# Mixing the MLP's two products tile by tile, with the second product one batch older

## The chip, the cores and the metric

One core of a Trainium2 chip runs the whole program. The metric is the device time of one execution in microseconds (us); each number quoted for a kernel is the median of its runs. Every run comes with the mean granted clock of TensorE (1.0 is full speed) and a state; for comparisons only runs of state "fast" are used (on one core, a run is slow when it is over 1.5% above the fastest of the same kernel). Ratios are computed as the mean time of one kernel's fast runs over the mean of the other's from the same rounds, so a ratio is not quite that of the two medians beside it.

## The reference

Attention with an added one in the softmax denominator, for 8 batches, 12 heads, 448 positions and 64 dimensions, followed by an MLP with a squared ReLU over the 3,584 resulting tokens.

```python
scores = scale * np.matmul(q, k.transpose(0, 1, 3, 2))
m = np.max(scores, axis=-1, keepdims=True)
e = np.exp(scores - m)
attn = e / (np.sum(e, axis=-1, keepdims=True) + np.exp(-m) + 1e-09)
attn_out = np.matmul(attn, v)
x = attn_out.transpose(0, 2, 1, 3).reshape(B * S, H * D)      # 3584 x 768
h = x @ w_in                                                  # 768 x 2048
r = np.maximum(h, 0.0)
out = (r * r) @ w_out                                         # 2048 x 768
```

## The kernel before

Attention runs in units of one batch and two heads, six units per batch (batch 0 has twelve, each of a part of the query positions). The MLP takes blocks of tokens: 128 and 256 from batch 0, then 512 and 384 in turn. While batch b's attention runs, TensorE also does the MLP of finished tokens: its matmuls are laid in five portions between the parts of each unit. A generator yields after each matmul, and `drain` takes matmuls from it until the portion's nanoseconds are used up.

```python
    def mlp_in(t0, n):                     # first product: 6 matmuls fill one PSUM tile (n >= 384)
        ...
        for f0 in range(0, NFFB, per):
            hp = m_psum.tile([128, 512], FP32, name="mp")
            ...                            # matmuls from win and xt, a yield after each
            nc.vector.tensor_scalar(out=rt[:, 0:m], in0=hp[:, 0:m], scalar1=0.0, scalar2=None, op0=ALU.max)
            nc.vector.tensor_mul(g[:, 0:m], rt[:, 0:m], rt[:, 0:m])

    def mlp_out(t0, n):                    # second product: 16 matmuls fill one PSUM tile
        ...
                op = m_psum.tile([128, 512], FP32, name="mp")
                ...                        # matmuls from g and wout, a yield after each
                nc.scalar.activation(out=ot[:, n0:n1], in_=op[:, 0:n1 - n0], func=AF.Copy, scale=OUT_SCALE)

    def drain(ns):
        while work and ns > 0:
            got = next(work[0], None)
            if got is None:
                work.pop(0)
            else:
                ns -= got
                left[0] -= got
    ...
    for i in range(NU + 1):                # one pass: scores of unit i, the rest of unit i - 1
        scores(u, et, 0)                   # first score group
        drain(share * 0.45)
        scores(u, et, 1)                   # second score group
        rcp = row_sums(prev, pes)
        values(prev, pet, xp, 0); values(prev, pet, xp, 1)
        drain(share * 0.15)
        for step in range(3):
            add_chunks(u, et, es, step)    # VectorE: sums of the exponentials
            drain(share * (0.15, 0.1, 0.15)[step])
        normalise(prev, xp, rcp)           # VectorE: writes one of xt's six chunks
        if i - 1 in ready:                 # a batch's last unit: its MLP becomes work
            for part in ready[i - 1]:
                queue(*part)
            share = left[0] / NPAIR
```

The pool `m_psum` has two buffers, shared by both products: a third tile can only begin when one of the two has been read out ("evicted"). VectorE evicts the first product (but for block 0), ScalarE the second; ScalarE also does all exponentials. I call the six passes that work on one block's MLP a stage.

The names in the profile lines: `qk` and `vn` are attention's operands, `sp` the scores, `et` their exponentials, `es` sums of these, `zp` the row sums, `rcp` their reciprocals, `xp` the values and `xt` the normalised output; `mp` is a tile of either product, `rt` and `g` its ReLU and the square, `ot` the output.

The softmax here doesn't subtract the row's maximum and nothing guards it: scores larger than these inputs give would overflow.

## Time and profile before

| | before |
|---|---|
| median time | 448.77 us (448.7 with later runs of the same rounds) |
| span in the profile | 445.8 us |
| TensorE busy, idle | 426.6 us, 19.2 us |
| TensorE's waits for VectorE's evictions of the first product | 5.3 us (4.8 + 0.5) |
| TensorE's waits for ScalarE's evictions of the second product | none |

TensorE's busy time is not its time at peak, and its idle time is real: a matmul that waits for a semaphore is not counted as busy. (A stop of a few tenths of a us can hide behind the end of the matmul before it, which the profile models.) In a kernel whose TensorE is 96% busy, the list of what TensorE waited for is the place to look, and the order in time around each wait says why it waited.

### The profile page before, as it was taken

Reading aid. Unit: us, or ns where it says so; the run is one execution under the profiler, and the core shown is the slowest. Engines: PE = TensorE matmul, PEld = TensorE weight load, DVE = VectorE, ACT = ScalarE, POOL = GpSimd, SP = SyncE. Lnnn points to the kernel's source line nnn. Section 1 sums busy time; section 2 is a strip of 40 time slices with the busy share of each in tenths; the row PEclk is TensorE's granted clock in tenths of the full one; section 3 lists DMA queues with packets and bytes.
Section 4 is the critical chain, followed back from the end, with each engine's and each line's share of the span. In section 5 each row is a group of like instructions: output and inputs, shape, how many; then the busy total and the mean of one; then the engine's idle time right before and its main releaser. Section 6 shows DMA issues by size and latency. Waiting matters only on the chain.

```text
span 445.8 us, 7533 instructions
## 1 busy us (share of the span) xinstructions
PE 426.6 (96%) x3147; PEld 228.7 (51%) x3147; DVE 244.7 (55%) x487; ACT 247.8 (56%) x361; POOL 33.8 (8%) x52
## 2 busy tenths in 40 slices
PE   8978899999999999999999989999999999999996
PEld 3556554544455545554455544654455545554454
DVE  3767683378722775258832487248662377428700
ACT  2888767754456646674456745764455655650011
POOL 8441100010000100010000100030000000000000
PEclk9999999999999999999999999999999999999999
DMA  9999999199021991279312793039902200010022
GB/s 171 197 197 204 208 202 197 52 191 216 1 64 46 198 179 33 71 124 207 79 37 71 116 217 79 37 62 206 178 1 72 71 1 1 37 37 35 1 71 71
DMA packets 78946, 47.22 MB, mean 106 GB/s; under 512 B 50624, under 2 KB 74944, under 8 KB 78528
## 3 DMA queue, kind: packets, MB, share of 16 engines
q0 software_dynamic: 24608, 22.40, 31.8%
q1 hardware_dynamic: 54304, 24.34, 23.9%
q8 instruction: 24, 0.39, 0.4%
q14 instruction: 10, 0.08, 0.1%
HBM read 45.71 MB, written 19.32 MB: 146 GB/s over the span
## 4 chain that ended last, share of the span: by engine, by line
PE 74%; DVE 17%; ACT 3%; issue 2%; DMA 2%; POOL 1%; ACTq 0%; POOLq 0%
PE mp L279 34%; PE mp L256 20%; PE xp L222 7%; PE sp L186 7%; DVE rt L265 7%; DVE es L199 4%; DVE g L267 3%; PE zp L230 3%; DMA kn<-in_k_dram 2%; ACT et L154 2%; PE sp L174 2%; DVE es L201 1%; DVE xt L242 1%; ACT lnz L233 1%; PE mp L146 1%
## 5 line engine op out<-in xcount | busy, mean ns | idle before, releaser
L154 ACT ACTIVATE et<-sp 112x896 f16<-112x896 f32 (+2 forms) x192 | 166.2, 913 | 125.4 <-PE sp L186 103.9
L256 PE MATMUL mp<-xt,win 128*128 128x512 f16 (+3 forms) x864 | 159.1, 332 | 8.3 <-DVE rt L265 4.8
L279 PE MATMUL mp<-wout,g 128*128 128x512 f16 (+1 forms) x896 | 154.2, 326 | 0.8 <-DVE rt L265 0.5
L256 PEld LDWEIGHTS <-win 128*128 128x128 f16 x864 | 77.3, 98 | 82.8 <-issue 25.7
L279 PEld LDWEIGHTS <-g 128*128 128x128 f16 x896 | 84.2, 98 | 64.6 <-issue 11.5
L199 DVE TENSOR_TENSOR es<-et 112x896 f16<-112x896 f16 x84 | 51.5, 621 | 106.3 <-ACT et L154 106.3
L265 DVE TENSOR_SCALAR rt<-mp 128x512 f16<-128x512 f32 (+1 forms) x120 | 76.0, 633 | 46.2 <-PE mp L256 43.5
L283 ACT ACTIVATE ot<-mp 128x512 f32<-128x512 f32 (+1 forms) x56 | 27.3, 487 | 64.5 <-PE mp L279 63.8
L267 DVE TENSOR_TENSOR g<-rt 128x512 f16<-128x512 f16 (+1 forms) x124 | 49.5, 399 | 7.0 <-ACT rt L263 2.8
L222 PE MATMUL xp<-et,vn 112*64 112x448 f16 (+2 forms) x432 | 45.5, 332 | 0.0
L186 PE MATMUL sp<-qk 64*112 64x224 f16 x576 | 42.8, 268 | 0.0
L186 PEld LDWEIGHTS <-qk 64*112 64x112 f16 x576 | 26.9, 127 | 25.4 <-issue 25.4
L233 ACT ACTIVATE lnz<-zp,one_b 128x448 f32<-128x448 f32 (+2 forms) x54 | 32.2, 596 | 1.9 <-PE zp L230 1.9
L242 DVE TENSOR_TENSOR xt<-xp,rcp 128x448 f16<-128x448 f32 (+2 forms) x54 | 30.5, 565 | 2.7 <-ACT rcp L234 2.7
L234 ACT ACTIVATE rcp<-lnz 128x448 f32<-128x448 f32 (+2 forms) x54 | 28.9, 535 | 1.7
L222 PEld LDWEIGHTS <-vn 112*64 112x64 f16 x432 | 24.0, 110 | 10.2 <-issue 0.2
L79 POOL DMA_DIRECT2D vn<-in_v_dram x10 | 8.9, 889 | 252.4 <-PE xp L222 239.6
L201 DVE TENSOR_TENSOR es<-es 112x896 f16<-112x896 f16 x42 | 26.2, 623 | 1.0
L230 PE MATMUL zp<-es,ones 112*64 112x448 f16 (+2 forms) x108 | 19.4, 356 | 1.0 <-DVE es L207 0.9
L174 PE MATMUL sp<-qk 64*112 64x192 f16 (+2 forms) x144 | 16.8, 308 | 1.6 <-ACT et L154 1.3
L363 PE MATMUL mp<-warm 128*128 128x512 f16 x31 | 10.7, 444 | 1.2 <-DVE warm L301 1.2
L174 PEld LDWEIGHTS <-qk 64*112 64x112 f16 x144 | 6.8, 124 | 9.4 <-issue 6.5
(32 smaller groups left out, 80.3 us busy)
## 6 DMA issues: line engine op xcount, KB each, us to landing
out_dram<-ot SPq DMA_DIRECT2D x12, 384.0 KB, 2.4
vn<-in_v_dram POOLq DMA_DIRECT2D x6, 672.0 KB, 8.8
stage_q<-in_q_dram POOLq DMA_DIRECT2D x5, 676.0 KB, 10.9
stage_k<-in_k_dram POOLq DMA_DIRECT2D x5, 676.0 KB, 13.7
win<-in_moe_w_in_dram POOLq DMA_DIRECT2D x8, 384.0 KB, 14.6
wout<-in_moe_w_out_dram POOLq DMA_DIRECT2D x4, 768.0 KB, 20.4
out_dram<-ot SPq DMA_DIRECT2D x8, 288.0 KB, 2.6
out_dram<-ot SPq DMA_DIRECT2D x8, 192.0 KB, 2.7
```

Of the source, the lines that this page charges most:

```text
L154: nc.scalar.activation(out=out_, in_=in_, func=AF.Exp, scale=scale)
L174: nc.tensor.matmul(sp[:, h, o:o + n], qk[r, 1, x + P * kk:x + P * kk + P], qk[r, 0, x + q0:x + q0 + n], start=True, stop=True)
L186: nc.tensor.matmul(sp[:, odd, h * (S // 2):(h + 1) * (S // 2)], qk[r, which, kx:kx + 2 * P - 1:2], qk[r, 0, x:x + S // 2], start=True, sto ...
L199: nc.vector.tensor_add(f[:, step], e[:, 2 * step], e[:, 2 * step + 1])
L222: nc.tensor.matmul(xp[64 * h:64 * h + 64, 0:n], vns[b][:, 2 * pr + h, kk, :], of_head(chunk(et, u, c, kk), u, h), start=(kk == 0), stop=(k ...
L230: nc.tensor.matmul(zp[64 * h:64 * h + 64, 0:n], ones, of_head(total, u, h), start=True, stop=True)
L233: nc.scalar.activation(out=lnz[:, 0:n], in_=zp[:, 0:n], func=AF.Ln, bias=one_b)
L242: nc.vector.tensor_mul(xts[b // 2][:, pr, c:c + n], xp[:, 0:n], rcp[:, 0:n])
L256: nc.tensor.matmul(hp[:, j * n:(j + 1) * n], win[:, dc, fb * 128:(fb + 1) * 128], xt[:, dc, x0:x0 + n], start=(dc == 0), stop=(dc == DCH - 1))
L265: nc.vector.tensor_scalar(out=rt[:, 0:m], in0=hp[:, 0:m], scalar1=0.0, scalar2=None, op0=ALU.max)
L267: nc.vector.tensor_mul(g[:, 0:m], rt[:, 0:m], rt[:, 0:m])
L279: nc.tensor.matmul(op[:, 0:n1 - n0], gt[fb][:, ts * 128:(ts + 1) * 128], wout[:, fb, n0:n1], start=(fb == 0), stop=(fb == NFFB - 1))
```

## The change

The intent is to spread VectorE's load: in place of a run of first-product tiles and then a run of second-product tiles, the tiles alternate. The second product needs all of a block's first product, so it comes from the block one batch older. Boilerplate is cut; every `yield` also gets a flag that marks the end of a tile.

```diff
+    def mixed(parts):
+        gens = [[0.0, total, gen] for gen, total in parts]
+        while gens:
+            g = min(gens, key=lambda g: g[0] / g[1])
+            for ns, end in g[2]:
+                g[0] += ns
+                yield ns
+                if end:
+                    break
+            else:
+                gens.remove(g)
...
-    ready = {NPAIR - 1: [(1, 0, 128)],
-             2 * NPAIR - 1: [(1, 128, 256), (2, 0, 128), (2, 128, 256)]}
-    t0 = 384
+    ready = {NPAIR - 1: [(1, 0, 128)], 2 * NPAIR - 1: [(1, 128, 256), (2, 0, 128)]}
+    last, t0 = (2, 128, 256), 384
     for b in range(1, B):
         n = 384 if b % 2 == 0 else 512
-        ready[(b + 2) * NPAIR - 1] = [(1, t0, n), (2, t0, n)]
+        ready[(b + 2) * NPAIR - 1] = [(1, t0, n), last]
+        last = (2, t0, n)
         t0 += n
...
-                for part in ready[i - 1]:
-                    queue(*part)
+                queue(ready[i - 1])
...
+    queue([last])
     drain(1e12)
```

More of the change, by code (lines that the diff above doesn't have):

```diff
@@ L258, in mlp_in @@
                     if j < per - 1 or dc < DCH - 1:
-                        yield n / 2.4
+                        yield n / 2.4, False
             m = per * n
@@ L269, in mlp_in @@
                 gt.append(g[:, j * n:(j + 1) * n])
-            yield n / 2.4
+            yield n / 2.4, True
     def mlp_out(t0, n):
@@ L281, in mlp_out @@
                     if fb < NFFB - 1:
-                        yield (n1 - n0) / 2.4
+                        yield (n1 - n0) / 2.4, False
                 nc.scalar.activation(out=ot[:, n0:n1], in_=op[:, 0:n1 - n0], func=AF.Copy, scale=OUT_SCALE)
                 if n1 < DM:
-                    yield (n1 - n0) / 2.4
+                    yield (n1 - n0) / 2.4, True
             c = t0 + ts * 128
@@ L296, in mlp_out @@
                 c += m
-            yield (DM - 512) / 2.4
+            yield (DM - 512) / 2.4, True
     warm = consts.tile([128, 512], FP16)
@@ L326, with queue @@
     work, left = [], [0.0]
-    def queue(part, t0, n):
-        work.append((mlp_in if part == 1 else mlp_out)(t0, n))
-        left[0] += (NFFB * DCH * n if part == 1 else n // 128 * NFFB * DM) / 2.4
+    def mixed(parts):
[9 more added lines that the diff above has]
+                gens.remove(g)
+    def queue(parts):
+        both = []
+        for part, t0, n in parts:
+            total = (NFFB * DCH * n if part == 1 else n // 128 * NFFB * DM) / 2.4
+            both.append(((mlp_in if part == 1 else mlp_out)(t0, n), total))
+            left[0] += total
+        work.append(mixed(both))
     def drain(ns):
```

## The prediction

> **What bounds the kernel now.** I read the page first, then the busy time by stage, the waits of TensorE stage by stage, the chain of waits, and the instructions in order of time around each wait. The page's engine line and the slices:
>
> ```profile
> PE 426.6 (96%) x3147; PEld 228.7 (51%) x3147; DVE 244.7 (55%) x487; ACT 247.8 (56%) x361; POOL 33.8 (8%) x52
> ...
> PE   8978899999999999999999989999999999999996
> ...
> DMA  9999999199021991279312793039902200010022
> ```
>
> TensorE is busy in 426.6 of 445.8 us, so a reordering can win at most the 19.2 us of idle time, and much of that is at the two ends. The DMA row matters later: the engines are full for the first seven slices (78 us), while weights, the first batches and the staged copy of batch 2 arrive.
>
> The busy time by stage (stretch, its length, then PE, PEld, DVE and ACT busy) shows where the idle time is:
>
> ```profile
> 0.00:44.00 44.00, 37.19 (x425) 22.65 (x425) 27.48 (x73) 31.74 (x51) 20.11 (x30) 1.00 1.30 192
> 44.00:90.00 46.00, 43.66 (x344) 25.24 (x342) 26.33 (x50) 33.62 (x50) 3.64 (x6) 1.00 0.92 162
> 90.00:145.00 55.00, 54.42 (x367) 27.34 (x366) 29.80 (x55) 29.75 (x42) 1.07 (x2) 1.00 0.53 105
> 145.00:194.00 49.00, 47.59 (x365) 26.04 (x363) 28.17 (x59) 30.68 (x44) 2.65 (x6) 1.00 0.57 110
> ...
> 421.00:446.00 25.00, 20.70 (x128) 12.27 (x126) 1.05 (x2) 3.92 (x8) 0.00 (x0) 0.98 0.20 64
> ```
>
> 6.8 us are lost before 44 us, 2.3 to 90 us, 4.3 at the very end (the last eviction and its store), and only 0.58 or 1.41 us in each middle stage, alternately for a block of 512 and of 384 tokens. What the idle time waits for, over the whole run:
>
> ```profile
> PE mp L256 <- DVE rt L265: 4.8, 13, 0.6
> ...
> PE mp L279 <- DVE rt L265: 0.5, 1, 0.5
> ```
>
> These 5.3 us are what mixing can win: the first product's PSUM tiles come one after another with two buffers, and VectorE, which also does the attention's additions, is sometimes late with an eviction. From 84 us on the waits by stage are 0.3 us in each 512 stage and 1.2 us in each 384 stage, three of each: 4.5 us. ScalarE, which evicts the second product, costs TensorE nothing in the second product's tiles before the change: no such wait is listed.
>
> **What the Trainium skill says.** The page "Perfetto Trace Analysis" (section Optimization Strategy) advises interleaving regimes whose most contended engine differs. That is the change's intent, and the trace agrees that the regimes differ: the DVE row of the slices swings between 2 and 8. The same page (Matmuls) says that accumulation groups should rotate through banks so that one group's eviction overlaps the next group's matmuls; here the pool has two buffers, so an eviction has exactly one other tile's duration to finish in. "TensorE: Matmul & The Clock Gate", section Back-to-back issue gap, gives N/2.4 + 2.5 ns for a warm matmul, 215.8 ns at 512 columns and 109.2 at 256; the last 128 matmuls, half of each, took 20.81 us in the chain of waits, 162.6 ns each, against a mean of 162.5: it agrees, and the tail has no slack. The same page (Why this matters for your kernels) warns that idle gaps over about 3 us let the clock drop to half; no gap as long is in the trace before (granted clock 1.00), but see below.
>
> **The change, part by part.**
>
> *1. Work.* The order of instructions of both programs shows 6,296 TensorE instructions in each, the same 864 and 896 matmuls. Nothing is added or removed; the clean tail after attention only grows by the second product of the 384-token block, 48 matmuls of 512 and 48 of 256, 15.6 us, which leaves the middle by as much. Sum: 0.
>
> *2. VectorE waits removed.* A first-product tile is now mostly followed by a second-product tile of 1.75 or 3.45 us (16 matmuls) instead of 0.98 or 1.30 us (6 matmuls). By the order of instructions some 5 or 6 of 16 tiles per stage still have only one such short tile before their buffer is needed. So I keep a third of the 4.5 us: minus 3.0 us.
>
> *3. ScalarE waits added.* A second-product tile is now followed by a first-product tile, so its eviction must be done in 0.98 or 1.30 us, not in 1.75 or more. ScalarE takes its work in order, behind the exponentials:
>
> ```profile
> 119.55 1.72 ACT L154 ACTIVATE et<-sp 112x896 f16<-112x896 f32 x2 [2.94 <-PE sp L186]
> 122.00 0.60 ACT L283 ACTIVATE ot<-mp 128x512 f32<-128x512 f32 x1 [0.73 <-PE mp L279]
> 123.32 1.72 ACT L154 ACTIVATE et<-sp 112x896 f16<-112x896 f32 x2 [0.72 <-PE sp L186]
> 124.93 0.64 ACT L233 ACTIVATE lnz<-zp,one_b 128x448 f32<-128x448 f32 x1
> 125.60 0.58 ACT L234 ACTIVATE rcp<-lnz 128x448 f32<-128x448 f32 x1
> 126.08 0.36 ACT L283 ACTIVATE ot<-mp 128x256 f32<-128x256 f32 x1
> ```
>
> The two score groups before these start at 119.10 and 122.88 us. So after a unit's first score group ScalarE is free for an eviction 0.45 + 1.61 = 2.05 us later, after the second (exponentials, logarithm, reciprocal) 126.08 - 122.88 = 3.2 us later; an eviction takes 0.60 us (512) or 0.38 us (256), and I allow 0.07 us for the signal. From the new order I took, for each second-product tile, how many matmuls after a score group it ends, at the times per matmul above. A tile stalls TensorE where this gives less room than the eviction needs. Example: in each 384 stage one 512 tile ends 0.96 us after the first score group; its eviction ends at 2.05 + 0.60 + 0.07 = 2.72; the buffer is wanted at 0.96 + 0.98 = 1.94: 0.78 us lost. Also in each 384 stage, a 256 tile ends at 0.75: 2.05 + 0.38 + 0.07 - 0.75 - 0.98 = 0.77. In two of the 512 stages, one tile ends 1.81 after the second group: 3.25 + 0.60 + 0.07 - 1.81 - 1.30 = 0.81. With one of 0.13 this is 3 x 0.78 + 3 x 0.77 + 2 x 0.81 + 0.13 = 6.4 us. The same count over the old order gives no stall at all, which is what the trace has. Plus 6.4 us.
>
> *4. Batch 2 comes too soon.* Batch 0's second half of the second product (256 tokens, 2 x 16 x (215.8 + 109.2) ns = 10.4 us) moves from the stage before batch 2's attention into the one after. Five sixths of it, 8.6 us by the new order, lay before batch 2's first scores, which start at 83.69 us and would then be reached at 75.1. Their operands come by transposed loads that don't depend on TensorE here: the staging copy is asked for at 48 us, before the two programs' orders part, and the loads stand so in the queue's order of time:
>
> ```profile
> 64.87 4.92 SPq L129 DMA_TRANSPOSE qk<-stage_q  x1
> 69.84 6.14 SPq L129 DMA_TRANSPOSE qk<-stage_k  x2
> 76.02 14.97 SPq L295 DMA_DIRECT2D out_dram<-ot  x6
> ```
>
> The last load is issued at about 72.9 and takes a median of 5.3 us in this stretch; the DMA's activity ends at 78.8 us. Before, that left 4.9 us to spare. Now TensorE reaches the scores at 75.1 (76 to 77 if the thinner stage meets a few short waits for exponentials) and waits to 79.0. Against work that only moved, this is 79.0 - 75.1 = 3.9 us lost, whether shown as one wait or partly as waits before it. Plus 3.9 us.
>
> Sum: -3.0 + 6.4 + 3.9 = +7.3 us on 448.8, so about 456 us, 1.6% more.
>
> **The rivals.**
>
> *A. The mixing wins.* If ScalarE's evictions are never late, part 3 is 0 and the result is 448.8 - 3.0 + 3.9 = 449.7 us. For it: ScalarE is only 56% busy. Against it: what counts is the one to two us of exponentials in front of an eviction, not the mean load. If the loads of batch 2 were also early enough, 446 us; no view gives more than 4.5 us to win in the middle, so faster by 2% (under 439.8) has nothing to come from.
>
> *B. VectorE stays the bound.* All tight tiles still wait: part 2 is near 0, and the result is 459 us. For it: the runs of two or three first-product tiles that are left. Against it: VectorE's load is spread and is 55% on average.
>
> *C. The gap lets the clock fall.* If the wait at 76 us is long enough for the clock gate, one half-speed window follows. An estimate from that page's 3.4 us window: up to 1.7 us more, so 458.
>
> *D. DMA hides it anyway.* If the loads land by 75 us, part 4 is 0 and the result is 452. The slices speak against it: the DMA engines are full until then.
>
> **Range and chances.** Part 4 is surest (3 to 4.5), part 3 least (2 to 9: each stall hangs on a few tenths of a us), part 2 between -4 and 0. Together 450.5 to 460 us, with 456 as the middle. 457.7 is the limit of 2%: I give 0.27 to slower, 0.72 to within 2%, 0.01 to faster.
>
> **What would show it.** Part 2: the waits of first-product matmuls for the VectorE eviction fall from 4.8 us to 1 to 2. Part 3: a new row of waits appears, matmuls of either product waiting for the ScalarE eviction, some 8 to 11 times, 0.8 us at most each, about 6 us in all; without it rival A holds. Part 4: one wait of score matmuls for a transposed load at 76 to 79 us, 2 to 4 us long, with their first start at 79 and not near 75. Rival C: the granted clock under 1.0 in that slice. The prediction would be wrong if score groups drift against the tiles so that other tiles than those counted meet the exponentials, or if the loads of batch 2 finish at another time than before.

## More of the kernel before

The wait list: its columns are the waiting engine and line, what ended the wait, us in total, number of waits, and the longest.

```profile
PE mp L256 <- DVE xt L242: 1.7, 2, 1.5
```

Both waits are in the first 50 us. After that TensorE never waits before the change for `xt`, the normalised attention output that the first product reads.

## The result

The changed kernel took 460.36 us in the median of 6 runs, the kernel before 448.7; the ratio is 1.025 (95% interval 1.0206 to 1.0295), slower. The runs fall in two groups: three at a granted clock of 0.993 to 0.996 took 458.4 to 459.0 us, three at 0.980 to 0.984 took 461.7 to 462.7. A second set of 5 runs, all at 0.991 or more, took 457.66 us, ratio 1.0198 (1.0158 to 1.0238). The kernel before has low-clock runs too (451.0 and 451.8 us at 0.989 in that set), so I quote the loss as about 9 us and don't explain the clock's part by the change.

The profile of the changed kernel that was taken first is one of the low-clock runs. These are its engine line and its clock row (tenths of full speed in 40 slices):

```profile
PE 434.9 (94%) x3147; PEld 234.0 (51%) x3147; DVE 245.6 (53%) x487; ACT 248.7 (54%) x361; POOL 33.2 (7%) x52
...
PEclk9969999999989999999999999999999999899999
```

TensorE does the same 3,147 matmuls but is busy 8.3 us longer: the clock was at half between 26 and 37 us, and for some 3 us at 132 and at 395. The second profile, of the unaltered changed kernel again (456.3 us, clock 0.996), has one short such stretch, 27.4 to 30.7 us, so I use that one for accounts of time. TensorE's main waits are the same in both; the lines that answer to those before, in the second profile:

```profile
PE mp L257 <- DVE xt L242: 8.3, 8, 2.1
PE mp L257 <- ACT ot L284: 2.9, 5, 0.6
PE mp L280 <- ACT ot L284: 1.8, 3, 0.6
...
PE mp L280 <- DVE rt L266: 0.6, 2, 0.3
```

(L257 and L280 are the two products' matmuls, L266 and L284 their evictions; before they were L256, L279, L265 and L283.) The waits for VectorE's evictions went from 5.3 to 0.6 us: that is what the change was for. In their place came 4.7 us for ScalarE's evictions, and 6.6 us more than before for `xt`.

To see where the 10.5 us between the two spans lie, I cut both profiles at batch 2's first scores that could go on, 83.69 us before and 77.59 us after. Columns: the stretch, its length, then the busy time of PE, PEld, DVE, ACT and POOL, the granted clock, and the share and GB/s of the DMA engines. Before:

```profile
0.00:83.69 83.69, 74.53 (x709) 44.09 (x709) 51.79 (x118) 59.99 (x91) 22.09 (x33) 1.00 1.17 185
83.69:445.80 362.11, 352.05 (x2441) 184.65 (x2440) 192.92 (x369) 187.84 (x270) 11.68 (x19) 1.00 0.42 88
```

After:

```profile
0.00:77.59 77.59, 69.39 (x655) 40.94 (x655) 50.37 (x115) 59.31 (x89) 21.59 (x33) 0.98 1.24 195
77.59:456.30 378.71, 360.24 (x2492) 190.52 (x2492) 195.02 (x373) 188.82 (x272) 11.69 (x19) 1.00 0.40 85
```

The change moves 8.56 us of matmuls past the cut (by count 26 of 512 columns and 27 of 256, at the prediction's 215.8 and 109.2 ns). In the second part TensorE is busy 8.2 us longer, so the work explains that; its idle time went from 362.11 - 352.05 = 10.1 us to 378.71 - 360.24 = 18.5 us, 8.4 us more. In the first part the cut came 6.1 us earlier instead of 8.56: 2.5 us lost there. These are not idle time, which is 77.59 - 69.39 = 8.2 us there against 83.69 - 74.53 = 9.2 before: TensorE is busy 3.4 us longer than the moved work leaves (69.39 against 74.53 - 8.56). The half-clock stretch of 3.3 us makes about 1.7 us of that (an estimate, half its length); the rest is not traced. So the loss is new idle time in the middle, and a smaller loss ahead of batch 2, mostly longer busy time in this profile.

**The stage start.** Here are TensorE's instructions around the longest wait for `xt` in the second profile (start, us, engine, line, operation, and in brackets idle time before it and what ended it):

```profile
124.73 0.59 PE L186 MATMUL sp<-qk 64*112 64x224 f16 x8
...
125.46 0.92 PE L222 MATMUL xp<-et,vn 112*64 112x448 f16 x8
126.32 0.82 PE L257 MATMUL mp<-xt,win 128*128 128x512 f16 x3
127.07 0.59 PE L186 MATMUL sp<-qk 64*112 64x224 f16 x8
127.60 0.99 PE L257 MATMUL mp<-xt,win 128*128 128x384 f16 x5
130.65 0.32 PE L257 MATMUL mp<-xt,win 128*128 128x384 f16 x1 [2.06 <-DVE xt L242]
```

After the old batch's last values only 3 matmuls of its MLP are left. The next stage's first tile, of the first product, runs 5 of its 6 matmuls and then needs the chunk of `xt` that VectorE is still to write. VectorE at that time:

```profile
127.18 0.69 DVE L266 TENSOR_SCALAR rt<-mp 128x512 f16<-128x512 f32 x1 [1.95 <-PE mp L257]
127.90 0.42 DVE L268 TENSOR_TENSOR g<-rt 128x512 f16<-128x512 f16 x1
128.25 1.15 DVE L199 TENSOR_TENSOR es<-et 112x896 f16<-112x896 f16 x2
...
129.98 0.62 DVE L242 TENSOR_TENSOR xt<-xp,rcp 128x448 f16<-128x448 f32 x1
```

The old stage's last tile is a first-product tile. Its eviction stands first in VectorE's order, and the additions and `xt` wait behind it; `xt` is done 5.9 us after the second score group began. At the same place before the change the old stage ends with second-product tiles, which ScalarE evicts, and there are more matmuls left:

```profile
142.25 0.59 PE L186 MATMUL sp<-qk 64*112 64x224 f16 x8
...
143.85 1.81 PE L279 MATMUL mp<-wout,g 128*128 128x256 f16 x15
145.59 0.59 PE L186 MATMUL sp<-qk 64*112 64x224 f16 x8
146.11 2.12 PE L256 MATMUL mp<-xt,win 128*128 128x384 f16 x12
```

VectorE, with no eviction in the way, ends `xt` at 145.70 + 0.62 = 146.32 us there, 4.1 us after the second score group, and TensorE goes through:

```profile
145.70 0.62 DVE L242 TENSOR_TENSOR xt<-xp,rcp 128x448 f16<-128x448 f32 x1
```

Why so little work is left at the end of a stage is in `drain`: a portion ends with a whole matmul, up to 0.22 us late, and the excess isn't taken off the next portion. A stage has 30 portions; at about 0.1 us each (an estimate, half of a matmul of 0.22 us) the work runs out some 3 us early, which is most of the 0.55 x 35.8 / 6 = 3.3 us that a stage's last four portions hold (35.8 us by the program's own count, columns / 2.4 ns for each matmul). This was so before, with 0.55 x 41 / 6 = 3.8 us in the longer stages, but there no stage start after 50 us waits for `xt`.

**ScalarE.** One of the 8 waits for an eviction, TensorE first and then ScalarE:

```profile
148.01 1.14 PE L257 MATMUL mp<-xt,win 128*128 128x384 f16 x6
149.75 1.14 PE L257 MATMUL mp<-xt,win 128*128 128x384 f16 x6 [0.60 <-ACT ot L284]
```

```profile
147.49 1.72 ACT L154 ACTIVATE et<-sp 112x896 f16<-112x896 f32 x2 [2.67 <-PE sp L186]
149.10 0.60 ACT L284 ACTIVATE ot<-mp 128x512 f32<-128x512 f32 x1
```

A second-product tile ended at 148.0 us, 1 us after a score group had begun at 147.05. Its eviction began only at 149.10, behind two exponentials, and the tile after next waited for its buffer until 149.75.

### The profile page after: what moved, and what is told of

It is laid out like the page before. It is cut to its first block, busy times and chain, and to the rows that moved or that the text cites. A ratio compares the mean times of both kernels' runs of the same rounds, so it can differ in the third digit from the quotient of the medians.

```text
span 461.0 us, 7517 instructions
## 1 busy us (share of the span) xinstructions
PE 434.9 (94%) x3147; PEld 234.0 (51%) x3147; DVE 245.6 (53%) x487; ACT 248.7 (54%) x361; POOL 33.2 (7%) x52
## 4 chain that ended last, share of the span: by engine, by line
PE 78%; DVE 8%; ACT 7%; issue 3%; DMA 2%; POOL 1%; ACTq 0%; POOLq 0%
PE mp L280 33%; PE mp L257 26%; PE sp L186 7%; PE xp L222 7%; ACT et L154 5%; DVE rt L266 3%; PE zp L230 3%; DVE es L199 2%; PE sp L174 2%; DMA kn<-in_k_dram 2%; DVE g L268 1%; DVE xt L242 1%; ACT ot L284 1%; ACT lnz L233 1%; PE mp L146 1%
## 5 line engine op out<-in xcount | busy, mean ns | idle before, releaser
L257 PE MATMUL mp<-xt,win 128*128 128x512 f16 (+3 forms) x864 | 166.7, 336 | 11.5 <-DVE xt L242 8.3
L280 PE MATMUL mp<-wout,g 128*128 128x512 f16 (+1 forms) x896 | 163.2, 330 | 2.7 <-ACT ot L284 1.8
L266 DVE TENSOR_SCALAR rt<-mp 128x512 f16<-128x512 f32 (+1 forms) x120 | 76.3, 636 | 132.9 <-PE mp L257 131.1
L280 PEld LDWEIGHTS <-g 128*128 128x128 f16 x896 | 85.4, 99 | 76.7 <-issue 23.4
L257 PEld LDWEIGHTS <-win 128*128 128x128 f16 x864 | 79.4, 99 | 74.8 <-issue 16.9
L284 ACT ACTIVATE ot<-mp 128x512 f32<-128x512 f32 (+1 forms) x56 | 27.3, 488 | 65.1 <-PE mp L280 65.0
L222 PE MATMUL xp<-et,vn 112*64 112x448 f16 (+2 forms) x432 | 46.5, 338 | 1.3 <-DVE xt L242 1.3
L186 PEld LDWEIGHTS <-qk 64*112 64x112 f16 x576 | 27.2, 128 | 28.1 <-issue 28.0
L174 PE MATMUL sp<-qk 64*112 64x192 f16 (+2 forms) x144 | 18.5, 325 | 1.6 <-ACT et L154 1.3
L174 PEld LDWEIGHTS <-qk 64*112 64x112 f16 x144 | 7.6, 131 | 10.3 <-issue 7.7
```

The source lines that it names most:

```text
L174: nc.tensor.matmul(sp[:, h, o:o + n], qk[r, 1, x + P * kk:x + P * kk + P], qk[r, 0, x + q0:x + q0 + n], start=True, stop=True)
L186: nc.tensor.matmul(sp[:, odd, h * (S // 2):(h + 1) * (S // 2)], qk[r, which, kx:kx + 2 * P - 1:2], qk[r, 0, x:x + S // 2], start=True, sto ...
L222: nc.tensor.matmul(xp[64 * h:64 * h + 64, 0:n], vns[b][:, 2 * pr + h, kk, :], of_head(chunk(et, u, c, kk), u, h), start=(kk == 0), stop=(k ...
L257: nc.tensor.matmul(hp[:, j * n:(j + 1) * n], win[:, dc, fb * 128:(fb + 1) * 128], xt[:, dc, x0:x0 + n], start=(dc == 0), stop=(dc == DCH - 1))
L280: nc.tensor.matmul(op[:, 0:n1 - n0], gt[fb][:, ts * 128:(ts + 1) * 128], wout[:, fb, n0:n1], start=(fb == 0), stop=(fb == NFFB - 1))
```

## The experiments

Nine kernels ran, eight of them new and all correct, each with 5 rounds against the kernel before. "Changed" in the table is the second set of the changed kernel.

| run | median us | ratio to before (95%) |
|---|---|---|
| `again` (changed) | 457.66 | 1.0198 (1.0158 to 1.0238) |
| `out_first` | 454.79 | 1.0131 (1.009 to 1.0172) |
| `carry` | 450.99 | 1.0049 (1.0016 to 1.0082) |
| `lag_only` | 453.69 | 1.0114 (1.0079 to 1.015) |
| `first_stage` | 456.89 | 1.0188 (1.0138 to 1.0238) |
| `finish` | 446.24 | 0.995 (0.9912 to 0.9987) |
| `finish_out_first` | 442.84 | 0.9884 (0.9856 to 0.9912) |
| `all_three` | 441.0 | 0.9831 (0.9793 to 0.9869) |
| `before_carry` | 447.1 | 0.9978 (0.9932 to 1.0024) |

The theory: TensorE's new idle time comes from the stage starts, where `xt` is late and the work has run dry, and from ScalarE's evictions behind exponentials, with the early arrival at batch 2 as a third. The rivals: only one of these matters, or the lag itself costs, or the half-clock stretches do.

**The changed kernel again.** No edit.

> The changed kernel unaltered, for a second profile and more runs at known clocks. Theory (waits at the stage starts, for the xt of the last pair, carry the loss; half-clock windows come on top): 458 to 459 us where the granted clock is 0.996, 461 to 463 where it is 0.98; the first-product matmuls wait about 8 us for VectorE's xt, in 6 to 8 waits, and about 5 us for the ScalarE evictions. Step 4 of the prediction: in a run whose start is at full clock the first scores of batch 2 wait 3 to 4 us for a transposed load; if they do not, that step is wrong, not only hidden by the slow start of the first profile.

457.66 us. The main waits came out the same to a tenth. The loss is there at full clock too: its one run at clock 1.0 took 457.16 us, against 447.3 to 448.1 for the before runs at 0.999 to 1.0. So the clock is not the cause of the loss; in the first set it added to it. At batch 2 the first scores did wait for a transposed load:

```profile
77.59 0.59 PE L186 MATMUL sp<-qk 64*112 64x224 f16 x7 [0.34 <-DMA qk<-stage_k]
```

That is 0.34 us and not 3 to 4; but this run's half-clock stretch at 27.4 to 30.7 us had already made TensorE late. So the expectation's condition, a start at full clock, was not met, and of the cut's 2.5 us above at most about 0.8 is left for the early arrival in this profile. Whether a run at full clock waits longer instead is not shown.

**A second-product tile first at each stage start.**

```diff
-        for part, t0, n in parts:
+        for part, t0, n in reversed(parts):
```

> Each stage starts with a tile of the second product (which needs nothing new) in place of one of the first product (which needs the xt just normalised). Theory that the stage starts carry the loss: the 8 us of waits for xt fall under 2, no half-clock window at the stage starts, 450 to 452 us. Rival that the ScalarE evictions carry it: their waits stay near 5 us and the time stays at 456 or more.

454.79 us, more than expected, though the mechanism held. The wait list:

```profile
PE mp L257 <- ACT ot L284: 4.3, 8, 0.6
PE mp L280 <- DMA wout<-in_moe_w_out_dram: 3.4, 2, 2.7
PE mp L280 <- ACT ot L284: 1.8, 3, 0.6
...
PE mp L257 <- DVE xt L242: 1.5, 1, 1.5
```

The waits for `xt` fell from 8.3 to the 1.5 us of the very first stage, as the theory says. But batch 0's stage now began with `wout`, whose load had not landed (3.4 us, a wait I had not foreseen, with a half-clock stretch from 56 to 60 us after it), and three more tiles ended at a bad moment for ScalarE (6.1 us in place of 4.7). Less `xt` 6.8, plus 3.4 and 1.4, is 2.0 us less; the medians differ by 2.9.

**Portions kept to their length.**

```diff
     def drain(ns):
+        ns -= over[0]
         while work and ns > 0:
...
+        over[0] = -ns if work else 0.0
```

> The portions of MLP work laid between attention's parts are kept to their length: what one portion takes too much is taken off the next, so that a stage's work is not used up before its last portions. Theory that the work runs dry before the stage ends and leaves TensorE nothing but a tile that needs xt: the waits for xt fall from 8 to under 3 us, 451 to 454 us. Rival (the order at the stage start alone matters): waits for xt stay above 5 us and the time at 457 or more.

450.99 us, as expected. Most of the loss goes with a change that only hands the excess of a portion to the next:

```profile
PE mp L257 <- DVE xt L242: 4.5, 5, 1.5
PE mp L257 <- ACT ot L284: 3.7, 7, 0.8
PE sp L186 <- DMA qk<-stage_k: 3.4, 2, 2.6
```

After 84 us, 3.0 us of waits for `xt` are left, by the same view cut to that stretch. Because the portions are shorter, less MLP work lies ahead of batch 2, TensorE reaches its scores at about 73.0 us, and the wait for the transposed loads is now plain: 0.8 and 2.6 us. A half-clock stretch follows it, from 76.2 to 80.0 us: rival C of the prediction, at the place that it named.

**The lag alone, not mixed.**

```diff
-                queue(ready[i - 1])
+                for part in reversed(ready[i - 1]):
+                    queue([part])
```

> One part of the change alone: the second product runs one batch late, but before the first product of the stage and not mixed with it. Theory: no waits for xt at the stage starts and none for ScalarE's evictions; the VectorE eviction waits come back (about 5 us); what is left against the kernel before is the early arrival at batch 2 (0 to 4 us): 449 to 453 us. Rival (the lag itself costs, by clock or by loads): 455 us or more.

453.69 us, slightly over what was expected. No wait for `xt` at later stage starts, none for ScalarE's evictions, 2.5 us for VectorE's. Cut at its batch 2 (79.5 us), the second part has 372.50 - 361.86 = 10.6 us of idle time against 10.1 before. Its loss is ahead of batch 2: 79.5 + 8.56 - 83.69 = 4.4 us, with 2.6 us of waiting for `wout` and a granted clock of 0.96 up to there. That wait is not the lag's: this edit, like `out_first`, also starts each stage with the second product, batch 0's too. For the same reason it doesn't tell mixing from order at the stage starts. It shows that the lag itself costs nothing in the middle: the middle's 8.4 us come from the mixed order, first-product tile first.

**Batch 0's second product in its own stage.**

```diff
-    last, t0 = (2, 128, 256), 384
+    last, t0 = None, 384
...
-        ready[(b + 2) * NPAIR - 1] = [(1, t0, n), last]
+        ready[(b + 2) * NPAIR - 1] = [(1, t0, n)] + ([last] if last else [])
...
                 queue(ready[i - 1])
+                if i == 2 * NPAIR:
+                    queue([(2, 128, 256)])
```

> The changed kernel with one part undone: all of batch 0's second product runs in its own stage, as before the change, so that TensorE comes to batch 2 no earlier than before. Theory (the early arrival at batch 2's loads costs 2 to 4 us): 453.5 to 455.5 us, no wait of score matmuls for a transposed load. Rival (the early arrival costs nothing, all is in the waits for xt and ScalarE): 457 to 458 us, as the changed kernel.

456.89 us: hardly better than the changed kernel, and nearer to the rival. The wait for the transposed loads is gone, but the profile has half-clock stretches at 12 to 16 and 29 to 33 us, and in this order two other kinds of waits were larger than in the changed kernel (ScalarE's evictions 5.2 us, score matmuls for exponentials 1.4 us), while those for `xt` were smaller (6.5 us). The clock doesn't decide it: the one run of each kernel at clock 1.0 took 456.75 us here and 457.16 in the changed kernel. So undoing the early arrival gained at most about 1 us, and this experiment doesn't resolve what it costs. `finish_out_first` and `all_three` below come closer.

**Second-product tiles finished ahead of a score group.** On top of `carry`; each yield also tells what is left of an open second-product tile (`rest`).

```diff
-        while work and ns > 0:
+        while work and (ns > 0 or 0 < rest[0] <= finish):
...
-            drain(share * 0.45)
+            drain(share * 0.45, 1200)
...
-            drain(share * (0.15, 0.1, 0.15)[step])
+            drain(share * (0.15, 0.1, 0.15)[step], 1200 if step == 2 else 0)
```

> The kernel of the run carry, and a portion that would stop within 1.2 us of the end of a second-product tile finishes it, so that ScalarE gets the eviction ahead of the next exponentials. Theory (the evictions wait behind the exponentials): the 3.7 us of waits for ScalarE evictions in carry go to under 1, and the time from 451.0 to 447 to 448.5 us. Rival (evictions put first delay the exponentials, and the wait moves to the score matmuls): 450 us or more, with new waits of score matmuls for the exponentials.

446.24 us, a little under what was expected. The waits for ScalarE's evictions are gone from the list (3.7 us in `carry`), and the time fell by 4.8. Not all of that need be theirs: in the profiles the wait for the transposed loads also fell, from 3.4 to 1.0 us, while smaller ones grew (`xt` by 0.5, `wout` by 1.1, exponentials by 1.0). The score matmuls' waits for exponentials are 1.4 us, all on line 174, that is in the first two batches; the rival's new waits did not come. So those evictions were late because of what stood ahead of them in ScalarE's order, not because ScalarE had too much to do: its busy time is 249.3 us here and 248.7 in `carry`.

**The same with a second-product tile first from batch 1 on.**

```diff
-        for part, t0, n in parts:
+        for part, t0, n in (parts if parts[0][1] < 384 else reversed(parts)):
```

> The kernel of the run finish, with a second-product tile first at each stage start from batch 1 on: all_three without the part that puts batch 0's second product back in its own stage. Theory: against finish (446.2) the waits for xt at the stage starts go, about 3 us: 443 to 444 us; what then separates it from all_three (441.0) is the early arrival at batch 2 alone, 2 to 3 us, and its wait of score matmuls for a transposed load is still there. Rival (the early arrival costs nothing once the rest is mended): 441 to 442 us.

442.84 us, a little under what was expected: the remaining waits for `xt` at the stage starts go (3.5 us after 84 us in `finish`), and 3.4 us with them. Between 90 and 440 us the profile of this run lists no wait of TensorE at all. One wait for a transposed load is left, 1.1 us, at batch 2.

**All remedies.** `finish_out_first` and `first_stage` together.

> All remedies together: portions kept to their length, a second-product tile first at each stage start (but in batch 0's own stage), batch 0's second product in its own stage, second-product tiles finished ahead of the score groups. Theory (the four waits are separate and add up): waits for xt under 2 us (the first stage's 1.5 stays), none for ScalarE evictions or for the transposed loads, 440 to 443.5 us, so 1 to 2% under the kernel before. Rival (the waits replace each other): 446 us or more.

441.0 us, as expected, 1.7% under the kernel before. Its longest waits are all in the first stages:

```profile
PE mp L280 <- DMA wout<-in_moe_w_out_dram: 2.6, 1, 2.6
...
PE mp L257 <- DVE xt L242: 1.5, 1, 1.5
```

Against `finish_out_first` it is 1.8 us faster by the medians and 0.0053 by the ratios, 2.4 us: an estimate of the early arrival's cost once the other waits are away. It is a rough one, for the two ran in different calls and the intervals of their ratios just overlap. The profiles place 1.3 us ahead of batch 2: its scores go at 77.21 us in `finish_out_first` with 8.57 us of work moved past them, and at 84.50 here; 1.1 of it is the listed wait.

**Control: the kernel before with its portions kept to their length.** The edit of `carry`, in the kernel before.

> Control: the kernel before with its portions kept to their length, nothing else. If the running dry of a stage's work cost the changed kernel alone, this one is within 1.5 us of before (447 to 450; the count of the order gives 3 short ScalarE waits of 0.4 us). If the kept portions are a gain of their own, 446 us or less, and carry's gain is not the changed kernel's fault mended.

447.1 us, ratio 0.9978, an interval that holds 1. So keeping the portions is worth little to the kernel before and 6.7 us to the changed one: it mends what the mixed order made fragile. It leaves the 5.1 us of waits for VectorE's evictions (4.6 and 0.5) that only mixing takes away, and `all_three`, which mixes, is 6.1 us faster.

## Why the prediction was right or wrong

The measured 460.36 us lies just above the range's top of 460.0, and the second set's 457.66 inside it; with ratios, 1.025 and 1.0198 stand against the predicted 1.016. The first set is slower by over 2%, to which I had given 0.27; the second set's interval spans the limit. The direction was right and part of the mechanism, but that the sum came near was luck: missing terms made up for two that were too large.

| term | predicted us | measured us |
|---|---|---|
| VectorE waits removed, after batch 2's start | -3.0 | -3.9 (4.5 to 0.6) |
| ScalarE waits added | +6.4 | +4.7, 8 waits of 0.6 |
| early arrival at batch 2 | +3.9 | +2.5 lost ahead of batch 2, about 1.7 of it a half-clock stretch; 0.3 listed as a wait |
| waits for `xt` at stage starts | not in the sum | +6.6, six waits |
| values, row sums and scores waiting | not in the sum | +2.1, of it 1.6 in the last pass of attention |

The measured terms without the early arrival add up to 9.5 us for the middle, against 8.4 us of new idle time there; the list puts each wait down to one releaser, and the 1.1 us of other idle time that fell is not traced.

- **Work (step 1)** held: the same matmuls, and TensorE's busy time past the cut grew by 8.2 us, against 8.56 us of moved work. "Sum: 0" was true of the work and was where the prediction went wrong, by the 6.6 us of waits for `xt` that the runs showed: it did not ask what stands at the seam where one stage's work ends and the next begins. The order of instructions that I counted for step 3 shows it (three matmuls, a score group, then a whole first-product tile), so the wait could have been seen beforehand: I looked at each second-product tile's room and not at the first-product tile's input.
- **Step 2** held: I had left the tight first-product tiles a third of the 4.5 us, and they cost 0.6. Rival B is out.
- **Step 3** held in kind, place and number: two waits in each of the three 384 stages and one in each of two 512 stages, 8 where 9 were counted (the ninth was to be 0.13 us), at 0.6 us and not 0.78. The size was off by the time that matmuls spend between a tile's last and the next tile's wait: the six matmuls after it took 1.14 us with their end, and I had 0.98. (In the third term I also used 3.25 us where the lines shown give 3.20.) Rival A, that evictions are never late, is out. The `finish` run shows the cause.
- **Step 4** held in kind and was too large: the loads let the scores go at 77.6 us and not at 79.0, so its size was 2.5 at most in place of 3.9. I had read the end of all DMA activity, 78.8 us, as the loads' end, but output writes issued from 76.02 us are in it; the issue at 72.9 and the median of 5.3 us give 78.2. In the changed kernel half-clock stretches near the start take up most of the 2.5; the pair at the end of the experiments puts the cost at 1.8 to 2.4 us, roughly. Rival D, that the loads hide it anyway, is close to true in such runs.
- **Rival C** (the clock) did not come at the wait for batch 2 in the changed kernel: the half-clock stretches followed the waits at 25, 130 and 393 us, and not in every profile (the wait at 25 us is there before the change too). In `carry`, where the wait for batch 2 was 0.8 and 2.6 us long, it did come. Whether the new waits make them more frequent is open: three of the changed kernel's first six runs were at 0.984 or less, none of its next five, and two of 11 before runs beside `all_three` were at 0.981 (one of them counted as slow).

## What to carry to other kernels

When work from a new batch is queued behind other work, ask for the first instruction at the seam what it needs and how much independent work is left to cover it; start with whatever needs nothing new. With two buffers, an eviction has only the next tile's time: interleaving cut it here from 1.75 us or more to 0.98 or 1.30 for the second product. What stood ahead of the eviction in its engine's order then mattered, and not that engine's load (248.7 and 249.3 us with and without the waits); finish a tile just ahead of a burst on the evicting engine and not just after. If filler work is cut into portions, carry each portion's excess to the next, or it runs out before the end.

## What the Trainium skill lacked or had wrong

- "TensorE: Matmul & The Clock Gate", Back-to-back issue gap: it gives about 131 ns per matmul of 512 columns as what a real stream of weight loads and matmuls sustains. Here, at the end of the kernel before (from 400.18 us), 96 such matmuls with their weight loads took 20.72 us in the chain of waits, 215.8 ns each, which is the page's formula for an isolated matmul.
- The same page, Why this matters for your kernels: its row on throughput drops warns of idle gaps over about 3 us. Half-clock stretches of about 3 us, once 10, began after waits of 1.5 us (at 25 us), 2.06 us (at 130 us) and 2.0 to 2.7 us (for `wout`, in four runs), and in other runs the waits at 25 and 130 us had no such effect. The page's section on a second failure mode says that frequent short idles can do this too, but gives no length.
- "Perfetto Trace Analysis", Optimization Strategy: it advises interleaving regimes with different contended engines and names no cost. Interleaving here took 3.9 us of waits away and put 4.7 us of eviction waits behind the other engine's work, and 6.6 us at the seams, until both were mended.
